# Attention and token mixing with their turns in groups of four to five units, the left-over tokens' product on all 128 rows, and a smaller transfer scratch for GpSimd

## The chip, the core and the metric

The kernel runs on one core of one Trainium2 chip. The metric is the device time of the whole program in microseconds (us). TensorE (PE in the profile, PEld for its weight loads), VectorE (DVE), ScalarE (ACT) and GpSimd (POOL) compute; SyncE (SP) issues most DMAs.

## What is computed

An attention with exponential random features feeds a mixer of two two-layer perceptrons, one over the tokens and one over the channels. Batch 8, 8 heads, 576 tokens of 64 channels, 128 features, token width 256, channel width 1536:

```python
def phi(x):
    proj = np.einsum('bhsd,df->bhsf', x, w_phi)
    proj = proj - np.max(np.abs(proj), axis=-1, keepdims=True)
    return np.concatenate([np.exp(proj), np.exp(-proj)], axis=-1)
q_p, k_p = (phi(q), phi(k))
kv = np.einsum('bhsf,bhsd->bhfd', k_p, v)
z = np.sum(k_p, axis=2)
x = einsum(q_p, kv) / (einsum(q_p, z) + 1e-06)      # heads side by side: 512 channels
h = np.maximum(xt @ w_tok1, 0.0) @ w_tok2           # xt: x with tokens last
u = x + h.transpose(0, 2, 1)
out = u + np.maximum(u @ w_ch1, 0.0) @ w_ch2
```

The mixers' weights arrive as float64.

## The kernel before, in words

**Precision.** Most products run in float32r on numbers split in two: `hi` is a rounded copy, `lo` the rest (`split`, L54). `mm3` (L62) adds three products, hi·hi, hi·lo and lo·hi. `convert` (L99) makes such pairs from the float64 weights, with an absolute value and a copy on ScalarE, four operations on VectorE (L117 to L120) and a subtraction on GpSimd (L60) for each block of 512 columns; 24 such blocks hold the channel mixing's weights.

**Attention.** The work goes over 32 pairs of heads, four pairs to a batch entry. A pair has 576 tokens of two heads; a unit is 128 rows of them, so a head has four units, and the last 64 tokens of both heads are stacked into one more, the tail. `less_max` (L175) projects two units at a time, adds the high and low parts (`part`, `pk`, `pq`), reduces to the rows' largest magnitude (`mx`, L210) and subtracts it (`pm`, L218, on GpSimd). `keys` (L243) goes through a pair's nine units in five groups (2, 2, 2, 2 and the tail), exponentiates with both signs (L262) and adds up `kv` (`add_kv`, L273). `queries` (L300) goes through a pair in four pieces, by token half and head: a piece is projected, `turn`ed (L333: two transposes on TensorE, and for the first token half the tail's as a third, since each head needs its part of it; exponentials L347; split into `qh` and `ql` at L59 and L60), and multiplied with `kv` in `numerators` (L359, tile `pn`). The first four pairs (PLAIN) run in plain float32 with 64-row operands, subtract on VectorE or ScalarE and skip the splits.

**Token mixing** (`token_mix`, L400) runs twice for a batch entry, 16 times in all, on two pairs' channels. Each unit is transposed (`px`, L407), split (`xh`, `xl`, two buffers each) and multiplied with `w1` into `pa`. The left-over 64 tokens stand apart: their high parts fill rows 0 to 63 of `xs` and their low parts rows 64 to 127, against `w1_h` repeated in both halves (L416, 128 rows), and then the high parts alone against `w1_l` (L418, 64 rows); the two alternate for the two halves of the width, four products in all. Then come `ah`, `al` and the second product `ph`.

**Channel mixing** (`channel_mix`, L447) takes 18 chunks of 256 tokens: 144 products into `h`, 144 into `acc` for each.

**Order.** All of it is written as five generators that `weave` (L532) advances by shares of TensorE time (the numbers that they yield). The tile framework then reorders each engine's instructions by its own timeline, and every engine runs its list in order. PSUM banks: three of the tag `rest` serve the queries' projections, turns and numerators and, after the first batch entry, the token mixing; one each serves `keys`, `kv` and `h`, and two serve `acc`. `BORROWED` counts the plain query projections that alternate between the `h` and `keys` banks.

Of the kernel before, what the change touches and what calls it, by code (L numbers as in the profile page):

```python
# [41 lines left out]
def mixer_kernel(ctx, tc, qk, vm, vt, w_phi, w1, w2, wc1, wc2d, out):  # L42
# [11 lines left out]
    def split(hi, lo, raw, eng_hi, eng_lo):  # L54
        """hi + lo is each float32 value of raw exactly."""
        if eng_hi is nc.scalar:
            nc.scalar.copy(hi, raw)
        else:
            eng_hi.tensor_copy(hi, raw)  # L59
        eng_lo.tensor_tensor(lo, raw, hi.bitcast(F32), op=ALU.subtract)  # L60
# [534 lines left out]
```

## Time and profile before

| | |
|---|---|
| Median of three runs | 1184.18 us (1181.11 to 1188.29) |
| The profiled execution: its span, first to last instruction | 1182.1 us |
| Instructions | 24091 |
| TensorE / its weight loads busy | 96% / 93% |
| VectorE / ScalarE / GpSimd busy | 73% / 45% / 50% |

The profile gives no other time for its execution than the span; the median lies 2.1 us above it. A group's row has the line, engine, operation, output<-inputs, sizes and count, then the microseconds that the group kept its engine busy and the mean nanoseconds of one, then the idle time before it with what ended that. A window's row has each engine's busy time and its count of instructions. TensorE's matmuls are pipelined: one lasts some 280 ns in the records while the next starts after less than half of that, so its pace is read from starts, not from durations.

### The profile page before, as it was taken

The numbers are of one execution on the slowest core, as the hardware profiler recorded it, in microseconds if no ns is written. First come the engines' busy times: TensorE is split into PE (matmuls) and PEld (weight loads), VectorE is DVE, ScalarE is ACT, GpSimd is POOL, SyncE is SP. The second block draws the span as 40 slices with busy tenths as digits, with TensorE's granted clock in tenths as the row PEclk, the third lists the DMA queues.
The fourth block names the chain that finished last, engine by engine and source line by source line (L and its number), as shares of the span: only waits on it lengthen the run. The fifth ranks groups of instructions, "written<-read, shape, count | busy, mean of one in ns | idle before, by whom it ended". The sixth has DMA issues, their size and how long they took to land.

```text
span 1182.1 us, 24091 instructions
## 1 busy us (share of the span) xinstructions
PE 1140.1 (96%) x9032; PEld 1097.6 (93%) x9032; DVE 862.7 (73%) x1782; ACT 535.2 (45%) x1544; POOL 592.4 (50%) x739
## 2 busy tenths in 40 slices
PE   6999978999999999999999999999999999999998
PEld 6778877998999899999999999999999999999998
DVE  7997998868878787877878576684787878663111
ACT  5796655544444445444544353443443445431110
POOL 4345675755555655555646364563564655430000
PEclk9899998999999999999999999999999999999999
DMA  8541131111111011111111011110111110000000
GB/s 228 163 148 31 50 112 44 49 31 49 31 31 49 26 35 40 31 49 31 32 49 31 19 32 49 32 49 10 41 40 40 33 47 12 19 1 19 19 19 19
DMA packets 64149, 54.31 MB, mean 46 GB/s; under 512 B 43617, under 2 KB 55169, under 8 KB 64033
## 3 DMA queue, kind: packets, MB, share of 16 engines
q1 hardware_dynamic: 63824, 52.41, 15.4%
q8 instruction: 72, 1.18, 0.4%
q14 instruction: 45, 0.36, 0.1%
q0 software_dynamic: 208, 0.36, 0.1%
HBM read 43.32 MB, written 9.44 MB: 45 GB/s over the span
## 4 chain that ended last, share of the span: by engine, by line
PE 73%; DVE 15%; ACT 4%; issue 4%; POOL 3%; DMA 0%; SPq 0%; DVEq 0%; ACTq 0%; POOLq 0%
PE h L66 23%; PE acc L66 22%; PE pkv L284 7%; PE pn L66 6%; PE ph L66 4%; PE pa L66 3%; DVE qh L59 2%; PE pt L340 2%; PE ppq L196 2%; PE ppk L196 2%; DVE den L385 2%; DVE ql L60 1%; PE px L407 1%; DVE bitsc L119 1%; DVE bitsc L117 1%
## 5 line engine op out<-in xcount | busy, mean ns | idle before, releaser
L66 PE MATMUL acc<-gh,wc 128*128 128x256 f32 x1728 | 342.0, 283 | 1.5 <-POOL wc L60 1.0
L66 PEld LDWEIGHTS acc<-gh,wc 128*128 128x128 f32 x1728 | 275.3, 189 | 1.9 <-POOL wc L60 1.2
L66 PE MATMUL h<-uh,wc_h 128*128 128x256 f32 x864 | 247.0, 286 | 3.4 <-DVE gl L475 1.8
L66 PE MATMUL h<-uh,wc_l 128*128 128x256 f32 x864 | 246.0, 285 | 0.4 <-POOL wc_l L60 0.4
L66 PE MATMUL h<-ul,wc_h 128*128 128x256 f32 x864 | 245.8, 285 | 0.3 <-POOL ul L455 0.3
L66 PE MATMUL acc<-gl,wc 128*128 128x256 f32 x864 | 241.8, 282 | 1.1 <-DVE gl L475 1.1
L262 ACT ACTIVATE kp<-pmk 128x256 f32<-128x256 f32 (+1 forms) x320 | 109.4, 389 | 164.4 <-POOL pmk L218 156.9
L60 POOL TENSOR_TENSOR ql<-qf,qh 128x320 fp32r<-128x320 f32 (+1 forms) x112 | 104.2, 930 | 133.3 <-DVE qh L59 118.9
L66 PEld LDWEIGHTS h<-uh,wc_h 128*128 128x128 f32 x864 | 163.2, 189 | 5.3 <-DVE gl L475 2.2
L284 PE MATMUL pkv<-v,kp 128*128 128x65 f32 (+1 forms) x1152 | 162.8, 275 | 3.5 <-ACT kp L262 2.5
L66 PEld LDWEIGHTS h<-uh,wc_l 128*128 128x128 f32 x864 | 163.5, 189 | 0.7 <-POOL wc_l L60 0.7
L66 PEld LDWEIGHTS acc<-gl,wc 128*128 128x128 f32 x864 | 162.7, 188 | 1.4 <-DVE gl L475 1.3
L66 PEld LDWEIGHTS h<-ul,wc_h 128*128 128x128 f32 x864 | 163.3, 189 | 0.7 <-POOL ul L455 0.5
L284 PEld LDWEIGHTS pkv<-v,kp 128*128 128x128 f32 x1152 | 153.5, 197 | 8.4 <-ACT kp L262 5.1
L59 DVE CAST qh<-qf 128x320 fp32r<-128x320 f32 (+1 forms) x224 | 110.7, 509 | 43.2 <-ACT qf L347 37.7
L475 DVE SCALAR_TENSOR_TENSOR gl<-h,gh 128x512 fp32r<-128x512 f32 x108 | 73.5, 680 | 90.0 <-ACT gh L474 89.4
L385 DVE RECIPROCAL den<-den 128x320 f32<-128x320 f32 x64 | 124.6, 1947 | 1.6 <-ACT den L381 0.5
L347 ACT ACTIVATE qf<-pt 128x320 f32<-128x320 f32 (+1 forms) x256 | 92.1, 412 | 74.2 <-PE pt L340 69.0
L66 PE MATMUL pn<-qh,kv 128*128 128x320 f32 (+1 forms) x448 | 117.8, 300 | 1.4 <-DVE qh L59 0.7
L474 ACT ACTIVATE gh<-h 128x512 fp32r<-128x512 f32 x108 | 65.0, 602 | 115.2 <-PE h L66 113.2
L386 POOL TENSOR_TENSOR xt<-xt,den 128x320 f32<-128x320 f32 x64 | 53.3, 834 | 113.2 <-DVE den L385 95.7
L455 POOL TENSOR_TENSOR ul<-xt,uh 128x64 fp32r<-128x64 f32 (+3 forms) x120 | 61.5, 536 | 87.1 <-ACT uh L454 86.2
(113 smaller groups left out, 2400.9 us busy)
## 6 DMA issues: line engine op xcount, KB each, us to landing
raw<-in_qk SPq DMA_DIRECT2D x27, 576.0 KB, 3.8
rawc<-in_wc SPq DMA_DIRECT2D x24, 512.0 KB, 4.1
v<-in_vm SPq DMA_DIRECT2D x31, 256.0 KB, 3.4
out_x<-xt SPq DMA_DIRECT2D x12, 256.0 KB, 2.2
out_x<-xt SPq DMA_DIRECT2D x16, 192.0 KB, 2.0
raw<-in_w SPq DMA_DIRECT2D x8, 256.0 KB, 4.4
out_x<-xt SPq DMA_DIRECT2D x16, 128.0 KB, 1.9
pair<-in_qk SPq DMA_DIRECT2D x8, 160.0 KB, 4.6
```

The source lines that it names most:

```text
L59: eng_hi.tensor_copy(hi, raw)
L60: eng_lo.tensor_tensor(lo, raw, hi.bitcast(F32), op=ALU.subtract)
L66: nc.tensor.matmul(o, a, m, start=first and i == 0, stop=last and i == 2, skip_group_check=group_ok)
L196: nc.tensor.matmul(ps[:, i].rearrange("p two f -> p (two f)"), t[:, c:c + P], wp2.rearrange("p two f -> p (two f)"), start=True, stop=True)
L262: nc.scalar.activation(kp[:, :len(us), sg], pm[:, :len(us)], AF.Exp, scale=1.0 - 2.0 * sg)
L284: nc.tensor.matmul(o, kp[:, n, sg], v, start=g == 0 and n == 0 and sg == 0, stop=u is None, skip_group_check=True)
L347: nc.scalar.activation(full, src, AF.Exp, scale=1.0 - 2.0 * sg)
L385: nc.vector.reciprocal(den, den)
L386: nc.gpsimd.tensor_tensor(x, x, den, op=ALU.mult)
L455: nc.gpsimd.tensor_tensor(l[:, d:d + n], t[:, c, o:o + n], h[:, d:d + n].bitcast(F32), op=ALU.subtract)
L474: nc.scalar.activation(gh, ph, AF.Relu)
L475: nc.vector.scalar_tensor_tensor(gl, ph, 0.0, gh.bitcast(F32), op0=ALU.max, op1=ALU.subtract)
```

## The change

- **Groups.** `less_max` takes a whole group and projects it in steps of two units (four in the plain pairs), each added straight into `pm`; one reduction and one subtraction in place then serve the group. Keys have groups of 4, 4 and 1 units; queries have two pieces a pair, the first of 5 units (two of each head and the tail between them), the second of 4. The piece of five is turned with five transposes in two banks and split at 640 columns; both heads' numerators read their columns of it. `kp` becomes four units wide with a tile of its own for the tail, and `kv`'s sums of a pair are emitted in two runs.
- **Token mixing** turns units 0 and 1 together and 3 and 4 together (512 columns in one bank, one split); `xh` and `xl` have one buffer each, of twice the size, and `xs` shares `xh`'s.
- **Left-over tokens.** `w1_l` is repeated in rows 64 to 127 too (one more 64x256 copy on ScalarE), and its products run on all 128 rows of `xs`: low·low is now added as well.
- **Transfers.** `w_phi` and the first pair's values go by ScalarE's queue in place of GpSimd's, and GpSimd's DMA scratch is 1024 bytes.
- `BORROWED` is 10 in place of 18, since there are fewer projections.

```diff
+BORROWED = 10
+SCRATCH = 1024
...
-    nc.gpsimd.dma_start(wp[D:], w_phi)
-    nc.gpsimd.dma_start(wp[:D], w_phi)
+    nc.scalar.dma_start(wp[D:], w_phi)
+    nc.scalar.dma_start(wp[:D], w_phi)
...
-        nc.scalar.copy(w1_h[D:, 2], w1_h[:D, 2].bitcast(F32))
+        for w in (w1_h, w1_l):
+            nc.scalar.copy(w[D:, 2], w[:D, 2].bitcast(F32))
...
+        pm = wk.tile([P, 4 if kind == "k" else 5, F], F32, tag=f"pm{kind}", name=f"pm{name}")[:, :n]
+        mx = wk.tile([P, 5], F32, tag=f"mx{kind}", name=f"mx{name}")[:, :n]
+        step = 2 if base is None else 4
+        for at in range(0, n, step):
+            us = units[at:at + step]
+            m, part = len(us), slice(at, at + len(us))
+            tag = f"{name}_{at}"
...
+            for i, u in enumerate(us):
...
+            if base is None:
+                low = wk.tile([P, 2, F], F32, tag="part", name=f"part{tag}")[:, :m]
+                nc.scalar.copy(low, ps[:, :m, 1])
+                nc.vector.tensor_tensor(pm[:, part], ps[:, :m, 0], low, op=ALU.add)
+                continue
+            nc.vector.tensor_reduce(mx[:, part], ps[:, :m], axis=AX.X, op=ALU.max, apply_absolute_value=True)
...
         if base is None:
...
+            nc.vector.tensor_reduce(mx, pm, axis=AX.X, op=ALU.max, apply_absolute_value=True)
+            nc.gpsimd.tensor_tensor(pm, pm, mx.unsqueeze(2).to_broadcast([P, n, F]), op=ALU.subtract)
         return pm
...
-        groups = [[(0, 0), (0, 1)], [(0, 2), (0, 3)], [(1, 0), (1, 1)], [(1, 2), (1, 3)], [None]]
-        todo = None
+        groups = [[(j, u) for u in range(4)] for j in range(2)] + [[None]]
...
-                kp = wk.tile([P, 2, 2, F], F32, tag="kp", name=f"kp{i}_{g}")
+                if g < 2:
+                    kp = wk.tile([P, 4, 2, F], F32, tag="kp", name=f"kp{i}_{g}")
+                else:
+                    kp = wk.tile([P, 1, 2, F], F32, tag="kt", name=f"kp{i}_{g}", bufs=1)
                 for sg in range(2):
-                    nc.scalar.activation(kp[:, :len(us), sg], pm[:, :len(us)], AF.Exp, scale=1.0 - 2.0 * sg)
-                yield 0.22
-                if todo:
-                    add_kv(*todo)
-                    yield 0.82
-                todo = (i, g, us, kp, v_sb)
-        add_kv(*todo)
-        yield 0.82
+                    nc.scalar.activation(kp[:, :, sg], pm, AF.Exp, scale=1.0 - 2.0 * sg)
+                yield 0.12 * len(us)
+                if g == 1:
+                    add_kv(*todo.pop())
+                    yield 1.8
+                todo.append((i, g, us, kp, v_sb))
+            for t in todo:
+                add_kv(*t)
+            todo = []
+            yield 2.2
...
-        pieces = [(i, k, j) for i in range(B * NP) for k in range(2) for j in range(2)] + [None, None]
-        for piece in pieces:
+        groups = [[(0, 0), (0, 1), None, (1, 0), (1, 1)], [(0, 2), (0, 3), (1, 2), (1, 3)]]
+        for piece in [(i, k) for i in range(B * NP) for k in range(2)] + [None, None]:
             if split_up:
                 yield from until(lambda: split_up[0] in kvs)
-                numerators(*split_up)
-                yield 0.75
+                for j in range(2):
+                    numerators(*split_up[:2], j, split_up[2])
+                    yield 0.8
...
+                pm = less_max(ts, groups[k], f"q{i}_{k}", plain)
+                turned = (i, k, pm)
+                yield 0.12 * len(groups[k])
+    def turn(i, k, pm):
+        n = (5, 4)[k]
+        w = n * P
+        full = [wk.tile([P, 5 * P], F32, tag="qf", name=f"qf{i}_{k}{sg}")[:, :w] for sg in range(2)]
+        for at in range(0, n, 4):
+            m = min(n - at, 4)
+            ptr = ps_w.tile([P, 4, P], F32, **REST, name=f"pt{i}_{k}{at}")
+            for u in range(m):
+                nc.tensor.transpose(ptr[:, u], pm[:, at + u], ident)
+            for sg in range(2):
+                nc.scalar.activation(full[sg][:, at * P:(at + m) * P],
+                                     ptr[:, :m].rearrange("p u s -> p (u s)"), AF.Exp, scale=1.0 - 2.0 * sg)
+        if i < PLAIN:
+            return i, k, full
         qps = []
         for sg in range(2):
...
+            hi = wk.tile([P, 5 * P], F32R, tag="qh", name=f"qh{i}_{k}{sg}")[:, :w]
+            lo = wk.tile([P, 5 * P], F32R, tag="ql", name=f"ql{i}_{k}{sg}")[:, :w]
+            split(hi, lo, full[sg], nc.vector, nc.gpsimd if sg else nc.vector)
             qps.append((hi, lo))
-        return i, k, j, qps
+        return i, k, qps
...
+            cols = slice(j * w, j * w + w)
             if i < PLAIN:
-                nc.tensor.matmul(pn, w_hl[0], qps[sg], start=sg == 0, stop=sg == 1)
+                nc.tensor.matmul(pn, w_hl[0], qps[sg][:, cols], start=sg == 0, stop=sg == 1)
             else:
-                mm3(pn, w_hl, qps[sg], sg == 0, sg == 1)
+                mm3(pn, w_hl, [q[:, cols] for q in qps[sg]], sg == 0, sg == 1)
...
+        def turned(us):
+            px = bank(b, [P, len(us), 2, P], f"px{b}_{h}_{us[0]}", 1)
+            for n, u in enumerate(us):
+                s0, w, _ = UNITS[u]
+                k = 0 if s0 < SEG[1][0] else 1
+                o = s0 - SEG[k][0]
+                for c in range(2):
+                    nc.tensor.transpose(px[:w, n, c], xt[k][:, 2 * h + c, o:o + w], ident)
+            return px
+        for us in ((0, 1), (2,), (3, 4)):
+            px = turned(us)
+            if us == (2,):
+                xs = wk.tile([P, 2, 2, P], F32R, tag="xh", name=f"xs{b}_{h}", bufs=1)[:, 0]
+                nc.scalar.copy(xs[:D], px[:D, 0])
+                nc.vector.tensor_tensor(xs[D:], px[:D, 0], xs[:D].bitcast(F32), op=ALU.subtract)
+                x_all = xs.rearrange("p c d -> p (c d)")
                 for t in range(NT):
                     ts = slice(t * P, (t + 1) * P)
-                    nc.tensor.matmul(pa[:, t], w1_h[:, u, ts], x_all, start=False, stop=False,
-                                     skip_group_check=True)
-                    nc.tensor.matmul(pa[:, t], w1_l[:w, u, ts], x_hi, start=False, stop=False,
-                                     skip_group_check=True)
-                yield 0.6
+                    for w1 in (w1_h, w1_l):
+                        nc.tensor.matmul(pa[:, t], w1[:, 2, ts], x_all, start=False, stop=False,
+                                         skip_group_check=True)
+                yield 0.8
...
+            xh = wk.tile([P, 2, 2, P], F32R, tag="xh", name=f"xh{b}_{h}_{us[0]}", bufs=1)
+            xl = wk.tile([P, 2, 2, P], F32R, tag="xl", name=f"xl{b}_{h}_{us[0]}", bufs=1)
+            split(xh, xl, px, nc.scalar, nc.vector)
+            for n, u in enumerate(us):
+                for t in range(NT):
+                    ts = slice(t * P, (t + 1) * P)
+                    mm3(pa[:, t], (w1_h[:, u, ts], w1_l[:, u, ts]),
+                        [x[:, n].rearrange("p c d -> p (c d)") for x in (xh, xl)],
+                        u == 0 and t == 0, u == 4, group_ok=True)
+                yield 0.8
...
-    nc = bacc.Bacc("TRN2", target_bir_lowering=False, num_devices=1)
+    nc = bacc.Bacc("TRN2", target_bir_lowering=False, num_devices=1, dynamic_dma_scratch_size=SCRATCH)
```

TensorE in the first token mixing of batch entry 3 (`xs3_0`, the left-over tokens), before:

```order
L66 MATMUL pn14_00_6418<-qh14_001_6373,kv1_14_6267 128x320
L416 MATMUL pa3_0_6281<-xs3_0_6394,w1_h_86 128x256
L418 MATMUL pa3_0_6281<-xs3_0_6394,w1_l_87 128x256
L416 MATMUL pa3_0_6281<-xs3_0_6394,w1_h_86 128x256
L196 MATMUL ppk15_3_6642<-wp2_80,stk151_6218 128x256 x2
L418 MATMUL pa3_0_6281<-xs3_0_6394,w1_l_87 128x256
L407 MATMUL px3_0_3_6427<-ident_73,xt1_3_5479 128x128 x2
```

and now:

```order
L67 MATMUL acc4_0_5055<-gh4_5_5583,wc2_11_1991 128x256 x2
L206 MATMUL ppq14_1_2_5650<-wp2_80,stq141_5410 128x256 x2
L437 MATMUL pa3_0_5536<-xs3_0_5611,w1_h_86 128x256
L437 MATMUL pa3_0_5536<-xs3_0_5611,w1_l_87 128x256
L437 MATMUL pa3_0_5536<-xs3_0_5611,w1_h_86 128x256
L437 MATMUL pa3_0_5536<-xs3_0_5611,w1_l_87 128x256
L423 MATMUL px3_0_3_5658<-ident_73,xt1_3_4841 128x128 x4
```

The four products keep their place and number; the 64-row form (L418) is gone, and four transposes follow where two did.

TensorE at the turn of query pair 14's first token half (`pt14`, `pmt14` is the tail), before:

```order
L284 MATMUL pkv15_6412<-v1_97,kp15_0_6232 128x65 x2
L340 MATMUL pt14_00_6361<-ident_73,pmq14_00_6260 128x128 x2
L284 MATMUL pkv15_6412<-v1_97,kp15_0_6232 128x65
L340 MATMUL pt14_00_6361<-ident_73,pmt14_6249 128x128
L284 MATMUL pkv15_6412<-v1_97,kp15_0_6232 128x65
L284 MATMUL pkv15_6412<-v1_97,kp15_1_6388 128x65 x4
```

and now:

```order
L298 MATMUL pkv15_5328<-v1_97,kp15_0_5269 128x65 x8
L298 MATMUL pkv15_5328<-v1_97,kp15_1_5312 128x65 x8
L298 MATMUL pkv15_5328<-v1_97,kp15_2_5482 128x130 x2
L67 MATMUL pa3_0_5536<-xh3_0_0_5542,w1_h_86 128x256
L356 MATMUL pt14_00_5589<-ident_73,pmq14_0_5413 128x128 x4
L356 MATMUL pt14_04_5596<-ident_73,pmq14_0_5413 128x128
```

Before, head 0's turn stands here and head 1's, with the tail once more, follows 71 rows later; now both heads and the tail are turned at once, and all of `kv`'s sums of pair 15 stand together ahead of it.

VectorE at the very start (`k0` and `q0` are pair 0's keys and queries, `t0` its tail), before:

```order
L210 TENSOR_REDUCE mxk0_0_114<-ppk0_0_111 128x2
L60 TENSOR_TENSOR wp2_80<-wp_81,wp2_80 128x128
L218 TENSOR_TENSOR pmk0_0_116<-ppk0_0_111,mxk0_0_114 128x256
L210 TENSOR_REDUCE mxk0_1_153<-ppk0_1_150 128x2
L218 TENSOR_TENSOR pmk0_1_155<-ppk0_1_150,mxk0_1_153 128x256
L210 TENSOR_REDUCE mxq0_00_143<-ppq0_00_140 128x2
L210 TENSOR_REDUCE mxt0_123<-ppt0_121 128x1
```

and now:

```order
L61 TENSOR_TENSOR wp2_80<-wp_81,wp2_80 128x128
L216 TENSOR_REDUCE mxk0_0_112<-ppk0_0_0_113 128x4
L223 TENSOR_TENSOR pmk0_0_111<-ppk0_0_0_113,mxk0_0_112 128x512
L216 TENSOR_REDUCE mxk0_1_155<-ppk0_1_0_156 128x4
L223 TENSOR_TENSOR pmk0_1_154<-ppk0_1_0_156,mxk0_1_155 128x512
L216 TENSOR_REDUCE mxk0_2_278<-ppk0_2_0_279 128x1
```

Two groups of two units have become one of four, so that VectorE has one 512-column operation where it had two of 256. Over the whole program VectorE's list shrinks from 1783 instructions to 1411, ScalarE's from 1544 to 1326 and GpSimd's from 741 to 540, and the matmuls that wait for a semaphore from 1630 to 1178.

More of the change, by code (lines that the diff above doesn't have):

```diff
@@ L27 @@
 EARLY = 8
-BORROWED = 18
+BORROWED = 10
+SCRATCH = 1024
 STAGES = 4
@@ L193, in less_max @@
-        for i, u in enumerate(units):
-            t, c = (ts[1], 512) if u is None else (ts[u[0]], P * u[1])
-            if base is None:
-                nc.tensor.matmul(ps[:, i].rearrange("p two f -> p (two f)"), t[:, c:c + P],
-                                 wp2.rearrange("p two f -> p (two f)"), start=True, stop=True)
-            else:
-                rows = slice(base, base + D)
-                nc.tensor.matmul(ps[:, i, 0], t[rows, c:c + P], wp[rows], start=True, stop=True)
-        if base is None:
-            part = wk.tile([P, 2, F], F32, tag="part", name=f"part{name}")
-            nc.scalar.copy(part[:, :n], ps[:, :n, 1])
-            pr = wk.tile([P, 2, F], F32, tag="p", name=f"p{name}")
-            nc.vector.tensor_tensor(pr[:, :n], ps[:, :n, 0], part[:, :n], op=ALU.add)
-            pr, eng = pr[:, :n], nc.gpsimd
-        else:
-            pr, eng = ps[:, :n, 0], nc.vector
@@ L285, in add_kv @@
                                  skip_group_check=True)
-        if g < 4:
+        if g < 2:
             return
@@ L311, in queries @@
                 split_up = turn(*turned)
-                yield 0.25
+                yield 0.5
             turned = None
             if piece:
-                i, k, j = piece
-                if (k, j) == (0, 0):
-                    plain = 0 if i < PLAIN else None
+                i, k = piece
+                plain = 0 if i < PLAIN else None
+                if k == 0:
                     if i < PLAIN:
@@ L326, in queries @@
                     asked.add(i)
-                    tail = less_max(ts, [None], f"t{i}", plain)
-                    yield 0.11
-                pm = less_max(ts, [(j, 2 * k), (j, 2 * k + 1)], f"q{i}_{k}{j}", plain)
-                turned = (i, k, j, pm, tail)
-                yield 0.22
-    def turn(i, k, j, pm, tail):
-        w = SEG[k][1]
-        ptr = ps_w.tile([P, 3, P], F32, **REST, name=f"pt{i}_{k}{j}")
-        rows = [pm[:, 0], pm[:, 1]]
-        if k == 0:
-            rows.insert(2 * (1 - j), tail[:, 0])
-        for n, r in enumerate(rows):
-            nc.tensor.transpose(ptr[:, n], r, ident)
-        o = D if k == 0 and j == 1 else 0
-        src = ptr.rearrange("p u s -> p (u s)")[:, o:o + w]
+                pm = less_max(ts, groups[k], f"q{i}_{k}", plain)
@@ L401, in token_mix @@
         pa = bank(b, [P, NT, 256], f"pa{b}_{h}", 0)
-        for u, (s0, w, _) in enumerate(UNITS):
-            k = 0 if s0 < SEG[1][0] else 1
-            o = s0 - SEG[k][0]
-            px = bank(b, [P, 2, P], f"px{b}_{h}_{u}", 1)
-            for c in range(2):
-                nc.tensor.transpose(px[:w, c], xt[k][:, 2 * h + c, o:o + w], ident)
-            if w < P:
-                xs = wk.tile([P, 2, P], F32R, tag="xh", name=f"xs{b}_{h}")
-                nc.scalar.copy(xs[:w], px[:w])
-                nc.vector.tensor_tensor(xs[w:], px[:w], xs[:w].bitcast(F32), op=ALU.subtract)
-                x_all, x_hi = (z.rearrange("p c d -> p (c d)") for z in (xs, xs[:w]))
+        def turned(us):
[7 more added lines that the diff above has]
+            return px
@@ L418, in token_mix @@
-                    nc.tensor.matmul(pa[:, t], w1_l[:w, u, ts], x_hi, start=False, stop=False,
-                                     skip_group_check=True)
-                yield 0.6
-                continue
-            xh = wk.tile([P, 2, P], F32R, tag="xh", name=f"xh{b}_{h}_{u}")[:w]
-            xl = wk.tile([P, 2, P], F32R, tag="xl", name=f"xl{b}_{h}_{u}")[:w]
-            split(xh, xl, px[:w], nc.scalar, nc.vector)
-            for t in range(NT):
-                ts = slice(t * P, (t + 1) * P)
-                mm3(pa[:, t], (w1_h[:w, u, ts], w1_l[:w, u, ts]),
-                    (xh.rearrange("p c d -> p (c d)"), xl.rearrange("p c d -> p (c d)")),
-                    u == 0 and t == 0, u == 4, group_ok=True)
```

62 lines of the change are left out of this document (29 added, 33 removed).

## The prediction

> **What bounds the kernel now.** I read the page first, then busy time by stretches, then TensorE's and VectorE's rows in order of time.
>
> ```profile
> span 1182.1 us, 24091 instructions
> ...
> PE 1140.1 (96%) x9032; PEld 1097.6 (93%) x9032; DVE 862.7 (73%) x1782; ACT 535.2 (45%) x1544; POOL 592.4 (50%) x739
> ```
>
> TensorE is busy for 96% of the span, the others far less; where the 4% lie the stretches tell (busy time and count for PE, PEld, DVE, ACT, POOL, then TensorE's granted clock and the DMAs), cut where TensorE becomes full and after the last attention:
>
> ```profile
> 0.00:220.00 220.00, 191.31 (x1194) 165.66 (x1195) 196.49 (x384) 142.07 (x386) 128.66 (x139) 0.95 0.37 105
> 220.00:1100.00 880.00, 870.90 (x7175) 854.27 (x7175) 652.29 (x1377) 382.70 (x1137) 458.12 (x593) 1.00 0.12 33
> 1100.00:1176.00 76.00, 76.00 (x653) 76.00 (x652) 12.58 (x20) 10.42 (x22) 5.66 (x8) 1.00 0.05 15
> ```
>
> Counts tell the pace. With channel mixing alone (the last row) a matmul passes every 76/653 = 0.116 us. From 220 to 1100 us it is 880/7175 = 0.1226 us: TensorE bounds this stage, with (0.1226 - 0.1164) x 7175 = 45 us over the bare pace. Up to 220 us it is 0.184 us, and there another engine is full:
>
> ```profile
> 80.00:100.00 20.00, 18.93 (x114) 14.70 (x114) 16.77 (x30) 16.55 (x51) 10.93 (x11) 1.00 0.30 98
> 160.00:180.00 20.00, 15.14 (x115) 13.74 (x115) 19.94 (x34) 11.97 (x29) 13.17 (x15) 1.00 0.44 133
> 200.00:220.00 20.00, 17.85 (x141) 17.08 (x141) 19.87 (x32) 9.66 (x27) 18.82 (x20) 1.00 0.07 15
> 220.00:240.00 20.00, 20.00 (x172) 20.00 (x172) 16.09 (x35) 11.52 (x33) 12.01 (x17) 1.00 0.20 59
> ```
>
> VectorE (the third of the five) is full in two of these, with a dip around 80 to 100 us, with the attention of seven pairs and the weights' conversion; when that ends, TensorE is full. So two things count: TensorE's own work and its stalls after 220 us, and VectorE's work before.
>
> **The left-over product on 128 rows.** TensorE's rows around one of the 16:
>
> ```profile
> 269.25 0.31 PE L66 MATMUL pn<-qh,kv 128*128 128x320 f32 x1
> 269.40 0.28 PE L416 MATMUL pa<-xs,w_h 128*128 128x256 f32 x1
> 269.61 0.38 PE L418 MATMUL pa<-xs,w_l 64*128 64x256 f32 x1
> 269.92 0.39 PE L416 MATMUL pa<-xs,w_h 128*128 128x256 f32 x1
> 270.24 0.38 PE L418 MATMUL pa<-xs,w_l 64*128 64x256 f32 x1
> 270.55 0.33 PE L407 MATMUL px<-ident,xt 128*128 128x128 f32 x1
> ```
>
> From start to start the four take 0.21, 0.31, 0.32 and 0.31, together 1.15 us: each change between 128 and 64 rows costs. Four at the bare 0.1164 take 0.47, so 0.68 is saved. Thirteen of the sixteen lie in TensorE's stage: -8.8 us; the three before 220 us (2.0 more) count only at the edge. The Trainium skill's "TensorE: Matmul & The Clock Gate", section "Why this matters for your kernels", says that a single product with few rows takes the same time as one with all 128. By that this term were nothing and the median 1168. The 0.31 us contradict it: the rule speaks of a product by itself, and here the form changes each time. I go by the row and leave that result no chance. The copy of `w1_l` is one ScalarE operation at the start, where ScalarE has gaps: nothing; uncovered it costs what a ScalarE copy of that size does, 0.36 us (the last row of the rivals).
>
> **Fewer transposes.** The tail is turned once a pair in place of twice: 32 fewer, 28 of them in the float32r pairs.
>
> ```profile
> 302.62 0.27 PE L340 MATMUL pt<-ident,pmt 128*128 128x128 f32 x1
> 302.97 0.38 PE L340 MATMUL pt<-ident,pmq 128*128 128x128 f32 x2
> 303.31 0.27 PE L66 MATMUL h<-ul,wc_h 128*128 128x256 f32 x1
> 303.42 0.28 PE L66 MATMUL h<-uh,wc_l 128*128 128x256 f32 x1
> ```
>
> A second one adds 0.38 - 0.27 = 0.11 us, so 28 x 0.11 = -3.1 us (-3.5 if all count).
>
> **VectorE before 220 us.** What merging is worth:
>
> ```profile
> 5.71 0.42 DVE L218 TENSOR_TENSOR pmk<-ppk,mxk 128x256 f32<-128x256 f32 x1
> 6.05 0.41 DVE L210 TENSOR_REDUCE mxk<-ppk 128x2 f32<-128x256 f32 x1
> ...
> 11.45 0.68 DVE L119 SCALAR_TENSOR_TENSOR bits<-raw,bits 128x512 uint32<-128x512 uint32 x1
> 12.05 0.41 DVE L218 TENSOR_TENSOR pmk<-ppk,mxk 128x256 f32<-128x256 f32 x1
> ...
> 13.85 0.15 DVE L214 TENSOR_SCALAR nmxq<-mxq 128x2 f32<-128x2 f32 x1
> ```
>
> A 256-column operation holds VectorE 6.05 - 5.71 = 0.34 us and one of 512 12.05 - 11.45 = 0.60, so two made one save only 0.08. By the code, four plain pairs lose 8 reductions and 8 subtractions of keys, 8 reductions of queries and 8 sign changes (20 become 12); four more pairs' keys lose 8 reductions; three pairs' queries lose 9 reductions and 5 low parts; three token mixings 6 low parts. That is 52 x 0.08 = 4.2 us, and 8 x 0.15 = 1.2. The casts of `qh` are dearer; the first row is of the first 220 us, the second, of the whole run, is the nearest cast of 640 columns:
>
> ```profile
> L59 DVE CAST qh<-qf 128x320 fp32r<-128x320 f32 (+1 forms) x22 | 14.0, 657 | 0.6 <-ACT qf L347 0.5
> L170 DVE CAST stq<-raw 64x640 fp32r<-64x640 f32 x28 | 18.9, 675 | 0.0
> ```
>
> 22 at 14.0 us become 11 at 0.675, 7.4: -6.6. Together VectorE loses 12 us. Since it isn't full around 100 us, I take two thirds, -8, between 0 (the dip swallows it) and -15 (with the three left-over products and fewer stalls).
>
> **Stalls after 220 us.** Of the 45 us over the bare pace 8.8 are the left-over product; the 320-column products pass in 269.40 - 269.25 = 0.15, 0.034 over the pace, and there are by the code some 28 x 12 `pn` and 16 x 12 `ph`, about 450 of them in this stage: 15 us. Some 21 us are left for waits. The matmuls that wait fall from 1630 to 1178, by 28%: -6 us. Below: a remaining wait can be longer, since its producer is; above: -14.
>
> **The start.** ScalarE now issues five DMAs, and its own first work is queued behind them, with the waits of two for GpSimd's fills and for an earlier landing:
>
> ```profile
> 0.75 0.57 SPq L237
> ...
> 6.17 1.21 ACT L262 ACTIVATE kp<-pmk 128x256 f32<-128x256 f32 x3 [4.13 <-DVE pmk L218]
> ```
>
> No ScalarE issue is in the trace; SP's take about 0.6 us, so 3 us, then the waits, then the table load. ScalarE had 4.1 us idle there, which covers nearly all: +0.6, between 0 and +2. The scratch and the fewer ScalarE and GpSimd instructions are costed at nothing, since neither engine bounds a stage (GpSimd's 18.82 of 20 from 200 to 220 us comes nearest); if they count, it is as a gain.
>
> **Sum.** -8.8 - 3.1 - 8.0 - 6.0 + 0.6 = -25.3 us: a span of 1156.8. The median lies 2.1 above the span now: 1158.9, say **1159**. The bounds give -43.4 (10.9 + 3.5 + 15 + 14), a median of 1141, and -9.9 (8.8 + 3.1 - 2), one of 1174.
>
> **Rivals.** *Only TensorE's work counts*: the first stage is bound by how weights, loads and the first token mixing follow each other, and the waits that remain are the binding ones. For it: VectorE's dip at 80 to 100 us; against it: the full windows. -11.9 + 0.6 gives 1173.
>
> *GpSimd blocks VectorE's casts.* Casts alternate with GpSimd's subtractions:
>
> ```profile
> 300.59 0.26 DVE L59 CAST qh<-qf 128x320 fp32r<-128x320 f32 x1
> ...
> L59 DVE CAST qh<-qf 128x256 fp32r<-128x256 f32 x112 | 63.3, 586 | 21.7 <-ACT qf L347 17.5 <-PE pn L66 3.7
> L60 POOL TENSOR_TENSOR ql<-qf,qh 128x320 fp32r<-128x320 f32 x56 | 58.9, 1052 | 106.4 <-DVE qh L59 102.8 <-PE px L407 3.7
> ```
>
> An undisturbed cast takes 0.26 us even at 320 columns, the mean of the 256-column ones is 0.586: they are held 0.3 us. GpSimd's operations have 512 or 640 columns in place of 256 or 320, about 1.5 us (estimated from 1.05 at 320), so a cast could be held that long. In the first stage that is 11 x 1.5 = 16 us against the 22 x 0.3 = 7 now, which turns the -8 into about +1: 1168. Against it: half as many meetings. The Trainium skill's "SBUF — State Buffer", section "Who interferes with whom", says that whoever comes first holds the shared ports for its whole instruction; the trace agrees as far as the 0.3 us go, and by that rule alone this rival would be the forecast.
>
> *Slower: the token mixing's turns are no longer covered.* `xh` and `xl` have one buffer, shared with `xs`, so each of the three turns of a mixing must be consumed before the next is written, and copy and low part of 512 columns stand between. Their nearest rows:
>
> ```profile
> L434 DVE SCALAR_TENSOR_TENSOR al<-pa,ah 128x512 fp32r<-128x512 f32 x16 | 10.9, 680 | 1.6 <-ACT ah L433 1.6
> L433 ACT ACTIVATE ah<-pa 128x512 fp32r<-128x512 f32 x16 | 9.6, 600 | 3.4 <-PE pa L66 3.4
> L412 DVE TENSOR_TENSOR xs<-px,xs 64x256 fp32r<-64x256 f32 x16 | 6.7, 418 | 5.2 <-ACT xs L411 4.8
> L411 ACT CAST xs<-px 64x256 fp32r<-64x256 f32 x16 | 5.8, 364 | 7.6 <-PE px L407 7.6
> ```
>
> Two turns of 0.60 + 0.68 and one of 0.36 + 0.42 are 3.34 us a mixing, 53 us in sixteen. Uncovered by over 31/53, six tenths, it is slower by over 0.5%; at nine tenths, 48 - 25, 1207. Against it: between a turn and its product other matmuls still stand in TensorE's list, and today's turns cost it almost nothing (21 us for all waits together).
>
> **Chances.** Forecast 0.63, only TensorE's work 0.17, casts blocked 0.09, turns uncovered 0.06, and 0.05 for small gains and losses that cancel (about 1184). A measurement of this kernel tells some 0.5% from no change: faster is below 1178.3. The first three lie there save for a little of the second's upper end: 0.86; same 0.08, slower 0.06. The range goes from the forecast's lower bound to past the second case, 1140 to 1179.
>
> **What would show it.** Right: the four `xs` products 0.12 us apart; 32 fewer PE records; TensorE full from about 212 us; a pace of about 0.120 us in the middle stage. Wrong: PE waiting for `xh`, `xl` or `xs` by over 10 us in the sum of waits, VectorE's cast mean over 1.2 us, or TensorE not full before 220 us.

## The result, and the profile after

The changed kernel takes 1215.1 us (median of four runs, 1213.3 to 1216.4) against 1184.4 before: 2.4% slower, ratio 1.024 (95% interval 1.021 to 1.027). I had forecast 1159. Its profiled execution spans 1211.4 us, 29.3 more. One of the ten executions of experiment 2 below took 3367 us and is left out of its figures. The page of the changed kernel, span and busy time:

```profile
span 1211.4 us, 22768 instructions
...
PE 1137.8 (94%) x9000; PEld 1105.8 (91%) x9000; DVE 812.8 (67%) x1410; ACT 509.2 (42%) x1321; POOL 568.4 (47%) x538
```

Every compute engine has fewer instructions, 1323 fewer in all, and VectorE is busy for 50 us less. TensorE has its 32 matmuls less and is idle for longer. The stretches (columns as before) say where:

```profile
0.00:220.00 220.00, 187.05 (x1201) 169.24 (x1202) 196.26 (x324) 140.21 (x347) 127.40 (x117) 0.90 0.39 111
220.00:1100.00 880.00, 845.30 (x6894) 832.02 (x6893) 595.46 (x1052) 353.59 (x943) 434.75 (x411) 0.98 0.11 31
80.00:100.00 20.00, 11.93 (x60) 9.45 (x60) 19.88 (x26) 12.38 (x31) 12.98 (x10) 0.83 0.32 107
```

Up to 220 us nothing is lost: 1201 matmuls against 1194. From 220 to 1100 us 6894 pass where 7175 did, though VectorE is busy for only 595 us there in place of 652, and the granted clock is 0.98 in place of 1.00. The waits of TensorE, longest sums after 220 us (microseconds in total, times, the longest; `gh` and `gl` are the high and low parts of the channel mixing's `h`):

```profile
PE ppq L206 <- DVE xs L432: 9.6, 3, 3.2
PE h L67 <- DVE gl L495: 6.8, 9, 2.1
PE ph L67 <- DVE pmq L214: 5.1, 4, 1.5
...
PE acc L67 <- DVE gl L495: 2.3, 1, 2.3
```

Before, the two longest in this stage were:

```profile
PE h L66 <- DVE gl L475: 1.8, 3, 1.1
PE ppq L196 <- DVE xl L60: 1.3, 3, 0.5
```

From the starts of all matmuls I made one account of this stage, 220 us to the last matmul. A matmul's time is the distance to the next start; what is over the bare pace of its shape (0.1165 us for 256 columns, 0.147 for 320, about 0.11 for the smaller) is excess. What the rows leave of a column is the bare pace itself, 911 to 919 us. The experiments of the last three columns are told below.

| us | before | changed | experiment 5 | experiment 8 | experiment 11 |
|---|---|---|---|---|---|
| 220 us to the last matmul's start | 957.5 | 986.8 | 948.8 | 957.9 | 952.1 |
| excess over 0.25 us at once (stalls) | 13.4 in 24 | 46.2 in 55 | 14.0 in 25 | 28.2 in 30 | 27.9 in 41 |
| excess of matmuls at half clock | 0 | 13.9 | 0 | 5.3 | 3.6 |
| around the left-over products | 8.9 | 1.7 | 0.2 | 0.9 | 0.2 |
| all other excess | 16.0 | 10.0 | 15.2 | 7.5 | 9.8 |

So the loss is stalls (+32.8 us), and after them a halved clock (+13.9); the other rows and the bare pace give 17.4 back. VectorE is at work during 42.2 of the 46.2 us of stalls, 91%, where over the whole stage it is at work for 68%: TensorE mostly waits while VectorE is busy. The largest stall, which comes at 272, 544 and 979 us, in order of time in the changed kernel (`stq` are arriving queries, cast on VectorE):

```profile
272.06 0.90 DVE L60 CAST qh<-qf 128x640 fp32r<-128x640 f32 x2 [1.48 <-ACT qf L358]
...
272.52 0.36 ACT L431 CAST xs<-px 64x256 fp32r<-64x256 f32 x1 [0.32 <-PE px L423]
...
272.87 0.82 DVE L61 TENSOR_TENSOR ql<-qf,qh 128x640 fp32r<-128x640 f32 x1
...
273.03 2.04 POOL L61 TENSOR_TENSOR ql<-qf,qh 128x640 fp32r<-128x640 f32 x1 [11.07 <-DVE qh L60]
...
273.60 1.75 DVE L172 CAST stq<-raw 64x512 fp32r<-64x512 f32 x1
...
275.39 0.42 DVE L432 TENSOR_TENSOR xs<-px,xs 64x256 fp32r<-64x256 f32 x1
...
275.95 0.77 PE L206 MATMUL ppq<-wp,stq 128*128 128x256 f32 x2 [3.20 <-DVE xs L432]
```

The next projection (`ppq`) needs a bank of the tag `rest`, and that bank holds the left-over tokens' turn until VectorE has made `xs`. ScalarE's half was done at 272.88, so `xs` could run then. It runs at 275.39, because a low part of 640 columns and a cast stand ahead of it in VectorE's list. Before, the first left-over turn after 220 us went through at once:

```profile
267.22 0.36 ACT L411 CAST xs<-px 64x256 fp32r<-64x256 f32 x1 [0.31 <-PE px L407]
...
267.61 0.42 DVE L412 TENSOR_TENSOR xs<-px,xs 64x256 fp32r<-64x256 f32 x1
```

In the changed kernel the cast takes 1.75 us, where its shortest in this trace takes 0.37, and ends at 275.35, 0.28 us after GpSimd's subtraction of 2.04 us (275.07). That agrees with the rule that I quoted from the Trainium skill's "SBUF — State Buffer" ("Who interferes with whom"): who comes first holds the shared ports for the whole instruction. A second place, 19 us later:

```profile
290.67 0.37 ACT L213 COPY partq<-ppq 128x256 f32<-128x256 f32 x1
...
291.22 0.92 DVE L60 CAST qh<-qf 128x512 fp32r<-128x512 f32 x1
...
292.18 0.49 DVE L172 CAST stk<-raw 64x640 fp32r<-64x640 f32 x1
...
292.70 0.42 DVE L214 TENSOR_TENSOR pmq<-ppq,partq 128x256 f32<-128x256 f32 x1
...
293.27 0.36 PE L67 MATMUL ph<-w_h,ah 128*128 128x256 f32 x1 [1.53 <-DVE pmq L214]
```

The sum `pmq` that frees the bank had its input at 291.04 and ran 1.66 us later, behind two casts. In the groups of VectorE's casts these places hardly show (whole run, mean of one in ns):

```profile
L60 DVE CAST qh<-qf 128x512 fp32r<-128x512 f32 x56 | 37.4, 690 | 4.6 <-ACT qf L358 4.3
...
L60 DVE CAST qh<-qf 128x640 fp32r<-128x640 f32 x56 | 33.8, 635 | 26.9 <-ACT qf L358 26.9
L172 DVE CAST stq<-raw 64x512 fp32r<-64x512 f32 x28 | 19.2, 686 | 18.1 <-PE ppq L206 18.1
```

The clock around the first place (same columns as the stretches):

```profile
268.00:271.80 3.80, 3.80 (x32) 3.49 (x31) 1.60 (x4) 1.62 (x4) 0.00 (x0) 1.00 0.51 140
271.80:275.20 3.40, 0.95 (x8) 0.71 (x7) 3.14 (x4) 1.04 (x5) 2.04 (x1) 1.00 0.00 0
275.20:282.00 6.80, 6.05 (x27) 6.08 (x28) 4.81 (x11) 2.02 (x5) 3.85 (x3) 0.50 0.27 86
```

Eight matmuls pass in the 3.4 us of the stall, and the next 6.8 us run at half clock. There are eight stretches at half clock after 220 us, 37.5 us in all, and none before the change until the last matmul.

### The profile page after: what moved, and what is told of

Its sections match the earlier page's. It is cut to its first block, busy times and chain, and to the rows that moved or that the text cites. A ratio compares the mean times of both kernels' runs of the same rounds, so it can differ in the third digit from the quotient of the medians.

```text
span 1211.4 us, 22768 instructions
## 1 busy us (share of the span) xinstructions
PE 1137.8 (94%) x9000; PEld 1105.8 (91%) x9000; DVE 812.8 (67%) x1410; ACT 509.2 (42%) x1321; POOL 568.4 (47%) x538
## 3 DMA queue, kind: packets, MB, share of 16 engines
q1 hardware_dynamic: 63824, 52.41, 15.2%
## 4 chain that ended last, share of the span: by engine, by line
PE 64%; DVE 17%; ACT 5%; POOL 4%; DMA 4%; issue 4%; SPq 0%; POOLq 0%; DVEq 0%; ACTq 0%
PE h L67 19%; PE acc L67 19%; PE pkv L298 7%; PE pn L67 6%; DMA raw<-in_qk 4%; PE ph L67 3%; DVE qh L60 3%; PE pa L67 3%; POOL stq L173 2%; DVE ql L61 2%; DVE den L399 2%; PE pt L356 2%; PE ppk L206 1%; PE px L423 1%; DVE stq L172 1%
## 5 line engine op out<-in xcount | busy, mean ns | idle before, releaser
L67 PE MATMUL acc<-gh,wc 128*128 128x256 f32 x1728 | 332.4, 283 | 1.6 <-ACT gh L494 1.6
L67 PEld LDWEIGHTS h<-uh,wc_h 128*128 128x128 f32 x864 | 166.5, 193 | 11.3 <-DVE gl L495 10.2
L67 PEld LDWEIGHTS h<-ul,wc_h 128*128 128x128 f32 x864 | 166.5, 193 | 0.3 <-POOL ul L475 0.3
L298 PE MATMUL pkv<-v,kp 128*128 128x65 f32 (+1 forms) x1152 | 146.5, 279 | 1.9 <-ACT kp L274 1.5
L298 PEld LDWEIGHTS pkv<-v,kp 128*128 128x128 f32 x1152 | 140.8, 197 | 4.3 <-ACT kp L274 3.2
L61 POOL TENSOR_TENSOR ql<-qf,qh 128x640 fp32r<-128x640 f32 (+1 forms) x56 | 92.7, 1655 | 85.6 <-DVE qh L60 80.8
L274 ACT ACTIVATE kp<-pmk 128x512 f32<-128x512 f32 (+1 forms) x192 | 90.0, 517 | 90.7 <-POOL pmk L227 85.0
L173 POOL TENSOR_TENSOR stq<-raw,stq 64x512 fp32r<-64x512 f32 (+1 forms) x56 | 94.8, 1698 | 34.0 <-DVE stq L172 32.5
L173 POOL TENSOR_TENSOR stk<-raw,stk 64x512 fp32r<-64x512 f32 (+1 forms) x56 | 82.9, 1487 | 58.4 <-DVE stk L172 49.3
L67 PE MATMUL pn<-qh,kv 128*128 128x320 f32 (+1 forms) x448 | 107.6, 309 | 2.1 <-DVE pmq L214 1.4
```

Of the source, the lines that this page charges most:

```text
L67: nc.tensor.matmul(o, a, m, start=first and i == 0, stop=last and i == 2, skip_group_check=group_ok)
L173: nc.gpsimd.tensor_tensor(t[lo:lo + D], src, t[base:base + D].bitcast(F32), op=ALU.subtract)
L274: nc.scalar.activation(kp[:, :, sg], pm, AF.Exp, scale=1.0 - 2.0 * sg)
L298: nc.tensor.matmul(o, kp[:, n, sg], v, start=g == 0 and n == 0 and sg == 0, stop=u is None, skip_group_check=True)
```

## The experiments

Three theories stood at first: H1, GpSimd's longer subtractions hold VectorE's casts; H2, VectorE's list itself, with longer operations ahead of the short ones that free a bank; H3, the mixing's single buffers. H4, the chance of a reshuffled order, came with the first results. Ratios are against the kernel before, on the same chip.

**Experiment 1: the left-over product alone**, added to the kernel before.

```diff
-        nc.scalar.copy(w1_h[D:, 2], w1_h[:D, 2].bitcast(F32))
+        for w in (w1_h, w1_l):
+            nc.scalar.copy(w[D:, 2], w[:D, 2].bitcast(F32))
...
-                    nc.tensor.matmul(pa[:, t], w1_l[:w, u, ts], x_hi, start=False, stop=False,
+                    nc.tensor.matmul(pa[:, t], w1_l[:, u, ts], x_all, start=False, stop=False,
...
-                yield 0.6
+                yield 0.8
```

> The kernel before with one part of the change alone: the left-over tokens' four products on all 128 rows, with the copy of w1_l. Theories of the loss: H1, GpSimd's longer subtractions hold VectorE's casts and what stands behind them in VectorE's list; H2, VectorE's own longer operations stand ahead of the short ones that free a PSUM bank; H3, the mixing's single buffers xh, xl and xs. None of the three is touched here, so all expect the gain that the prediction gave this part: 8.8 to 11 us, 1173 to 1176 us against 1184, and the four products 0.12 us apart.

1188.9 us, ratio 1.0016 (0.9996 to 1.0037): no gain. Yet the excess around the products fell from 8.9 to 0.4 us; stalls after 220 us rose from 13.4 to 20.1, and TensorE was 4 us further behind by 220 us. The gain was made and given back elsewhere.

**Experiment 2: the mixing's groups alone**, in the kernel before (`token_mix` as changed, the low product with 64 rows).

```diff
-        for u, (s0, w, _) in enumerate(UNITS):
+        for us in ((0, 1), (2,), (3, 4)):
+            px = turned(us)
...
-            xh = wk.tile([P, 2, P], F32R, tag="xh", name=f"xh{b}_{h}_{u}")[:w]
+            xh = wk.tile([P, 2, 2, P], F32R, tag="xh", name=f"xh{b}_{h}_{us[0]}", bufs=1)
```

> The kernel before with the token mixing's turns in groups alone (512 columns in one bank, xh and xl with one buffer, xs in xh's), the left-over product still with 64 rows and the attention as before. H3: the loss is here, 1184 + 20 to 40, 1204 to 1224 us, with TensorE waiting for xs, xh or xl by over 10 us. H1 and H2: nothing much, 1181 to 1188 us, since the attention's operations keep their lengths.

1193.1 us, 1.0056 (1.0031 to 1.0081): a small loss, between the two ranges, and no waits for `xs`, `xh` or `xl` of note after 220 us (`pa` for `xh` 0.7 us, for `xl` 0.3). Of the 11.7 us that its traced execution is longer, 6 are lost before 220 us and 3 in stalls after it. H3 is not the cause of the 2.4%.

**Experiment 3: the attention's groups alone** (the changed kernel with `token_mix` as before, the last diff the other way round, and `w1_l` not repeated; the smaller scratch, the moved transfers and BORROWED stay as changed, and no run takes them apart from the groups).

> The changed kernel with the token mixing as it was before (units turned one by one, two buffers, the 64-row product): the attention's groups, the scratch and the moved transfers alone. H1 and H2: the loss is all here and the left-over product's gain is missing, so 1215 + 9 = 1224 us (1215 to 1230). H3: no loss, at most 1184 us.

1250.2 us, 1.0528 (1.049 to 1.0567). The loss is in the attention's part of the change, and larger without the mixing's part than H1 and H2 said.

**Experiment 4: GpSimd's long subtractions in pieces.**

```diff
-            split(hi, lo, full[sg], nc.vector, nc.gpsimd if sg else nc.vector)
+            nc.vector.tensor_copy(hi, full[sg])
+            cut = w // 2 if sg else w
+            for o in range(0, w, cut):
+                (nc.gpsimd if sg else nc.vector).tensor_tensor(
+                    lo[:, o:o + cut], full[sg][:, o:o + cut], hi[:, o:o + cut].bitcast(F32), op=ALU.subtract)
```

(`pm` likewise, two units at a time.)

> The changed kernel with GpSimd's long subtractions cut: ql in two halves of 320 or 256 columns, pm in pieces of at most two units (256 columns), so that no piece is longer than before. VectorE's and ScalarE's operations stay. H1: a cast is held half as long, TensorE's stalls of over 0.25 us after 220 us fall from 46 us to some 20, and with them the half-clock windows: 1185 to 1195 us. H2 and H3: 1211 to 1219 us, as the changed kernel (1215).

1213.5 us, 1.0218 (1.0187 to 1.0249), as the changed kernel. At the same place as above, GpSimd's two pieces and VectorE's list:

```profile
279.02 2.37 POOL L372 TENSOR_TENSOR ql<-qf,qh 128x320 fp32r<-128x320 f32 x2 [10.84 <-DVE qh L369]
...
278.86 0.82 DVE L372 TENSOR_TENSOR ql<-qf,qh 128x640 fp32r<-128x640 f32 x1
279.59 1.08 DVE L172 CAST stq<-raw 64x512 fp32r<-64x512 f32 x1
280.70 0.42 DVE L439 TENSOR_TENSOR xs<-px,xs 64x256 fp32r<-64x256 f32 x1
```

The cast ends while GpSimd is at its second piece. It takes 0.67 us less, and the stall shrinks from 3.36 to 2.69 us; the rest of the list stands. Over the stage stalls are 42.0 in place of 46.2 us, and before 220 us TensorE falls 6 us further behind than in the changed kernel, which hides what little was gained. The stalls were to fall to some 20 us by H1, so H1 as the whole cause falls.

**Experiment 5: the left-over product alone, in the old order.** Experiment 1 with the old yield:

```diff
-                yield 0.8
+                yield 0.6
```

> The left-over product on all 128 rows alone, as in the first experiment, but with that turn's yield kept at 0.6 in place of 0.8. The number only tells weave how to share TensorE's time; with 0.6 the instructions of TensorE, VectorE, GpSimd and SyncE stand in exactly the order of the kernel before, where with 0.8 TensorE shared only 5226 of 7216 rows of its list with it. H4 (the gain was there and a reshuffled order gave it back): the 8.8 to 11 us, a ratio of 0.991 to 0.993 against before. If instead the term itself was wrong (the 64-row products cost nothing that matters): 1.000.

1178.1 us, 0.9915 (0.9881 to 0.995). The four products now stand 0.12 apart:

```profile
269.58 0.28 PE L418 MATMUL pa<-xs,w_h 128*128 128x256 f32 x1
...
269.69 0.28 PE L418 MATMUL pa<-xs,w_l 128*128 128x256 f32 x1
...
269.81 0.29 PE L418 MATMUL pa<-xs,w_h 128*128 128x256 f32 x1
...
269.93 0.28 PE L418 MATMUL pa<-xs,w_l 128*128 128x256 f32 x1
```

The account's row for them goes from 8.9 to 0.2, no other row moves by over 0.8, and the stage ends 8.7 us earlier. So the term was right, and the order's number alone cost experiment 1 all of it.

**Experiments 6 and 7: one half of the attention's groups undone**: `keys` as before, then `queries` and `turn` as before (with BORROWED 18), all else as changed.

```diff
-        groups = [[(j, u) for u in range(4)] for j in range(2)] + [[None]]
+        groups = [[(0, 0), (0, 1)], [(0, 2), (0, 3)], [(1, 0), (1, 1)], [(1, 2), (1, 3)], [None]]
```

> The changed kernel with the keys' groups as before (2, 2, 2, 2 and the tail, sums of kv after each); queries, mixing and the rest as changed. H2 (long operations one behind the other in VectorE's list): the keys' part of it are reductions and GpSimd subtractions of 512 columns, the smaller share: 1200 to 1215 us. If the keys' lumps (18 sums of kv in two runs) were the cause: about 1185.

1207.4 us, 1.0159 (1.0122 to 1.0196).

```diff
-        for piece in [(i, k) for i in range(B * NP) for k in range(2)] + [None, None]:
+        pieces = [(i, k, j) for i in range(B * NP) for k in range(2) for j in range(2)] + [None, None]
+        for piece in pieces:
```

> The changed kernel with the queries as before (four pieces a pair, two units each and the tail, turned for each head; BORROWED 18); keys, mixing and the rest as changed. H2: the 640- and 512-column casts, low parts and reductions that stood ahead of xs, pm and gl in most long stalls are gone, so most of the loss: 1180 to 1192 us. If the queries' groups were not the cause: 1205 to 1220.

1194.8 us, 1.0061 (1.0036 to 1.0085), a little above what H2 said. Undoing the queries' groups takes away three quarters of the 2.4%, undoing the keys' a third.

**Experiment 8: the queries' high parts on ScalarE.**

```diff
-            split(hi, lo, full[sg], nc.vector, nc.gpsimd if sg else nc.vector)
+            split(hi, lo, full[sg], nc.scalar, nc.gpsimd if sg else nc.vector)
```

> The changed kernel with the queries' high parts (qh) cast on ScalarE in place of VectorE: 100 casts after 220 us, 62 us of VectorE's time there, leave its list, and with them what GpSimd holds of them; ScalarE, 358 of 905 us busy there, takes some 68 us more. H2: stalls of over 0.25 us after 220 us fall from 46 to under 25 us and the time to 1180 to 1195. If VectorE's list were not the cause: 1208 to 1220.

1185.7 us, 0.9987 (0.9962 to 1.0012): the 2.4% are made good, though not the groups' whole cost: the left-over product alone gave 0.9915 (experiment 5). Stalls after 220 us fall to 28.2, a little short of what was expected, where experiment 5 has 14.0.

**Experiment 9: as 8, with all low parts on VectorE** (`split(hi, lo, full[sg], nc.scalar, nc.vector)`).

> The changed kernel with the queries' high parts on ScalarE, as in the eighth experiment (1185.7 us), and both low parts (ql) on VectorE, so that GpSimd has no ql at all. VectorE has then 25 more operations of 640 and 25 of 512 columns after 220 us, at 0.82 and 0.62 us undisturbed some 36 us, and GpSimd loses 82 us of the operations that held VectorE longest. H1 (GpSimd's holds are the loss): below the eighth, 1172 to 1182. H2 (what stands in VectorE's list, however short each): above the eighth, 1190 to 1205.

1203.4 us, 1.0145 (1.0113 to 1.0176), as H2 said and against H1: the operations that held VectorE longest are gone, and it is slower, since two more long subtractions a pair stand in VectorE's list. Stalls after 220 us are 40.7 in place of 28.2 us. The longest waits of this kernel after 220 us:

```profile
PE ph L67 <- DVE pmq L214: 9.6, 4, 3.7
PE ppq L206 <- DVE xs L432: 9.3, 4, 2.5
```

They are the two places shown above for the changed kernel. Nor is it VectorE's load alone (the third of the five). From 220 to 1100 us, of experiment 8:

```profile
220.00:1100.00 880.00, 856.96 (x7130) 848.60 (x7129) 540.35 (x966) 413.21 (x1054) 422.19 (x414) 0.99 0.12 32
```

and of experiment 9:

```profile
220.00:1100.00 880.00, 846.50 (x6962) 837.79 (x6961) 579.01 (x1011) 411.22 (x1048) 354.95 (x363) 0.98 0.12 32
```

Between these two stalls rise with the load, and the changed kernel goes on from there (595.46 us of load, 46.2 of stalls). But the kernel before has more load than any of them, 652.29 us, and only 13.4 us of stalls, so the load alone doesn't make them.

**Experiment 10: experiment 5 with the queries' high parts on ScalarE**, in the kernel before.

```diff
-            split(hi, lo, full, nc.vector, nc.gpsimd if sg else nc.vector)
+            split(hi, lo, full, nc.scalar, nc.gpsimd if sg else nc.vector)
```

> The kernel before with the left-over product on 128 rows at the old yield (the fifth experiment, 1178) and its queries' high parts on ScalarE. The kernel before waits only 13.4 us in stalls of over 0.25 us after 220 us, 12.3 of them with VectorE busy. H1 and H2 alike: at most 5 to 8 us of that can be won, 1170 to 1176, and the order is reshuffled (TensorE shares 5654 of 7236 rows), which cost 10 us in the first experiment: 1170 to 1188.

1177.9 us, 0.9926 (0.9899 to 0.9952): nothing beyond experiment 5. Stalls after 220 us are 11.5 in place of 14.0 us, and by 220 us TensorE, in a new order, is 6 us further behind.

**Experiment 11: experiment 8 with the arriving casts on ScalarE too.**

```diff
-            nc.vector.tensor_copy(t[base:base + D], src)
+            nc.scalar.copy(t[base:base + D], src)
```

> The eighth experiment with the casts of keys and queries as they arrive (stk, stq) on ScalarE too, so that VectorE has no cast left in the attention. In the changed kernel stq stood for 1.75 us ahead of xs, where its shortest is 0.37. H2 and H1: another 10 us or so of the 28 us of stalls that the eighth has left: 1172 to 1182. If ScalarE becomes late in its place (it has some 55 us more after 220 us): 1186 to 1195.

1178.4 us, 0.9936 (0.9913 to 0.9958). VectorE's list at the same place as above:

```profile
265.05 0.83 DVE L61 TENSOR_TENSOR ql<-qf,qh 128x640 fp32r<-128x640 f32 x1 [1.86 <-ACT qh L58]
265.92 0.42 DVE L432 TENSOR_TENSOR xs<-px,xs 64x256 fp32r<-64x256 f32 x1
```

One operation is left ahead of `xs`, and TensorE's stall there is 1.0 us where it was 3.4 (0.8 and 1.6 at its other occurrences). Yet over the stage the stalls stay at 27.9 us, where experiment 8 has 28.2, and the 10 us fewer that I expected did not come: VectorE is at work during 17.5 us of the stalls in place of 23.3, but now TensorE also waits for ScalarE (`ah`, 2.9 us) and GpSimd (`stk`, 2.6). Of the gain over experiment 8 some 5 us lie before 220 us, where TensorE is ahead by that much, and 1.7 in the halved clock. So the time fell into the expected range by another way.

**Experiment 12: one number of the order changed** in the changed kernel (the left-over turn's yield 0.6 in place of 0.8).

> The changed kernel with one number changed: the left-over turn's yield 0.6, as before, in place of 0.8. Operations, sizes and engines are all those of the changed kernel; TensorE shares 5873 of some 6940 rows of its order. If the loss is the chance of one order (H4): it moves by 10 us or more, anywhere from 1195 to 1225. If it is the groups' operations themselves (H2): 1211 to 1219.

1217.4 us, 1.0262 (1.0229 to 1.0294). A second order with the same operations gives the same loss and 48.7 us of stalls, so it is hardly the bad luck of one order (H4), though experiments 1 and 5 show that a new order can cost 10 us.

**Experiments 13, 14 and 16: small groups, with all of the attention's casts on ScalarE**: in 13 experiment 10 with the cast of experiment 11, in 14 experiment 11 with `keys` as before, in 16 experiment 7 with both casts moved (the same lines as in the diffs above).

> The tenth experiment (the kernel before with the left-over product on 128 rows and the queries' high parts on ScalarE, 1177.9) with the arriving keys' and queries' casts (stk, stq) on ScalarE too. H2: little is left to win after 220 us (11.5 us of stalls, 9.0 with VectorE busy); before 220 us VectorE is full and loses a few us: 1168 to 1176. If the groups are worth something of their own when VectorE is relieved, this stays above the eleventh (1178.4) less the 1.5% between run and run: 1175 to 1185.

1173.0 us, 0.9890 (0.9867 to 0.9914), the lowest time of all, though the intervals of experiments 5 and 14 overlap with its own. Up to 220 us VectorE, full before, has 175.20 us to do in place of 196.49, and 1217 matmuls pass in place of 1194 (the gain over experiment 10 lies there; after 220 us stalls are 16.3 us, where that one has 11.5):

```profile
0.00:220.00 220.00, 195.75 (x1217) 172.41 (x1218) 175.20 (x347) 161.73 (x431) 127.19 (x141) 0.93 0.38 110
```

> The eleventh experiment (changed kernel, no casts on VectorE, 1178.4) with the keys' groups as before. In the sixth run the old keys' groups gave 8 us. H2: with VectorE relieved less is to be had, 1172 to 1178. If the keys' larger groups are good once VectorE is relieved: 1179 to 1188.

1175.2 us, 0.9916 (0.9899 to 0.9933).

> The seventh experiment (queries as before, keys and mixing in groups, 1194.8) with all of the attention's casts on ScalarE. H2: its 21.4 us of stalls after 220 us, 18.4 with VectorE busy, shrink by half and VectorE's full first stage gains: 1172 to 1182. If its loss is in the mixing's single buffers and the keys: 1188 to 1195.

1191.2 us, 1.0043 (1.0023 to 1.0063): a miss for H2. Stalls after 220 us are 25.5 in place of 21.4 us. The longest wait is for ScalarE, whose `gh` stands behind a moved cast (0.61 us) and two exponentials of the keys' group (1.15 us together):

```profile
PE acc L67 <- ACT gh L495: 4.9, 3, 2.2
```

The time lies in the range that was expected if the loss is in the mixing's single buffers and the keys; no run tells that from a late ScalarE.

With VectorE relieved, the groups of four and five (experiment 11) are no better than those of two (experiment 13).

**Experiment 15: experiment 3 with the queries' high parts on ScalarE.**

> The third experiment (attention's groups alone, token mixing as before, 64-row product, 1250) with the queries' high parts on ScalarE. H2 (the 1250 is VectorE's list once more, with 32 more low parts xl in it): 1195 to 1210, as the eighth run plus 9 for the product. If the turns one by one in the mixing are the cause (each waits for a bank of its own among three): 1225 to 1245.

1210.3 us, 1.0209 (1.0187 to 1.023): 40 of the 64 us come back, so most of experiment 3's loss is VectorE's list too. Against experiment 8 some 25 us are left: 9 for the left-over product, 8 more by which TensorE is behind at 220 us, and 6 more of stalls. Why the mixing's groups give some 15 to 25 us beside the attention's, and cost 7 alone (experiment 2), no run here settles.

## Why the prediction was wrong, point by point

- **Left-over product, -8.8.** Right: -8.7 in experiment 5's account, -10 in its time. In the changed kernel the excess around it fell by 7.2.
- **Transposes, -3.1.** The 32 records are gone, 3.5 us at the bare pace. No run isolates them.
- **VectorE before 220 us, -8.** Wrong by all of it. TensorE's lag behind the bare pace (the time less all matmuls so far at that pace) was 34.9 us at 60 us before and 28.2 now, a gain of 6.7; at 100 us it was 49.5 and 50.5, at 220 us 81.1 and 80.3. I had named the end at 0, that the dip around 80 to 100 us swallows it. VectorE is full there now (19.88 of 20) and TensorE passes 60 matmuls where it passed 114. The dip was filled by other work: between 80 and 100 us the weights' conversion takes 10 us of VectorE's time where it took 1, since it stands later in the new order. No run tests what it would be worth to move it back.
- **Stalls after 220 us, -6.** This is the step that failed: "the matmuls that wait fall from 1630 to 1178, by 28%: -6 us". The number of waits fell; the stalls over 0.25 us went from 24 to 55, and from 13.4 to 46.2 us, and the pace to 880/6894 = 0.128 us in place of the 0.120 that I had named. For "a remaining wait can be longer" I gave no price. It should have had one: VectorE runs its list in order, as the rows show, and what stands there ahead of a bank's release is 0.9, 0.8 and 1.75 us of casts and `ql` now.
- **The clock.** Not in the sum at all: 13.9 us of excess at half clock follow the stalls. That they follow from them is read from the traces (below); no run made a stall on purpose.
- **The start, +0.6.** The first matmul starts at 3.82 us, 3.92 before; nothing lost.
- **Rivals.** "GpSimd blocks VectorE's casts" had the right neighbour in the wrong stage, and as a price only the hold. In the stalls 15.6 of VectorE's 42.2 us are over the shortest time of the same operation; the rest is the list's plain length, and halving the holder (experiment 4) took 4 us off the stalls and nothing off the time. "Turns uncovered" had the sign: TensorE waits for `xs`, `xl` and `xh` by 14 us, over the 10 that I had set as its mark. But `xs` stood in VectorE's list rather than waited for a buffer, and the mixing's groups alone cost 7 us, not 53. The mark "VectorE's cast mean over 1.2 us" was not met (0.64 and 0.69 us): a mean over 112 casts doesn't show three of 1.75 us at the place where all wait.

What experiments don't tell apart: whether each operation's length does it, or that a group makes two casts, a low part and their followers ready at one moment. Both make VectorE's run ahead of a short operation longer. Open is also what would remove the 28 us of stalls that stay in experiments 8 and 11, twice those of the kernel before.

## What to carry to other kernels

Merging operations lowers an engine's load and count but lengthens the run of work that a short, urgent operation finds ahead of it in an in-order list. Where another engine is the bound, price the change by that run at the places where a PSUM bank is freed, not by the sum of busy time: here VectorE had 57 us less to do in the stage and TensorE lost 33 to stalls. Moving work off the crowded list (casts to ScalarE) was worth 2.5% where the change had cost 2.4%. And before a small change is judged by a scheduled program, hold the order: one planner's number hid a 0.85% gain.
